# Second layer of a feed-forward by seven block products for eight, with sums on GpSimd

## The chip, the core and the metric

The kernel runs on one core of a Trainium2 chip. A core has TensorE (PE: matmuls, with weight loads of its own, PEld), VectorE (DVE), ScalarE (ACT), GpSimd (POOL) and SyncE (SP), which here issues the DMAs. The metric is device time in microseconds (us), lower is better. Each engine takes its instructions in the order in which the program holds them, and waits on semaphores for the other engines.

## What is computed

Chunked attention (8 batches, 8 heads, 576 tokens, chunks of 64) makes 4608 tokens of 512 numbers; a two-layer feed-forward follows, which is most of the work:

```python
scores = scale * np.matmul(q_c, k_c.transpose(0, 1, 2, 4, 3))   # per chunk of 64
attn = softmax(scores)
x = np.matmul(attn, v_c)  # 4608 tokens x 512
h = x @ w_in              # 512 x 2048
g = h - np.tanh(h)
return g @ w_out          # 2048 x 512
```

All is in float32. The kernel splits each operand of a matmul into a high and a low part and adds three products (high by high, high by low, low by high).

## The kernel before

The tokens are cut into nine **groups** of four tiles of 128 tokens (`SIZES`; the code's `g` runs from 0 to 8, and "the fourth group" is `g` = 3). The hidden width of 2048 is cut into 16 **chunks** of 128. A step of a group is one chunk: `gemm1` makes h of the chunk, transposed (hidden width on the partitions, 512 tokens along the free side), in 12 matmuls of 512 columns into one bank `ph` of two; `shrink` makes g and its two parts: ACT tanh into `t` (L465), DVE `h - tanh` (L466), ACT the high part `gh` (L472), DVE the low part `gl` (L473); `gemm2`, two steps later (`LAG`), multiplies the parts by the chunk's 128 rows of w_out, 12 matmuls of 512 columns, into the four banks `po`, which sum over the 16 chunks. `finish` scales `po` into tiles and stores them.

Groups 0 and 1 work on operands in fp32r. In groups 1 and 2 `convert` makes fp16 parts of the weights of both layers; from group 2 on both layers run on fp16. While a group's feed-forward runs, the attention of the next group is spread between its steps (`interleaved`): splits of q, k and v (L295 on ACT, L296 on DVE), score products (L306), maximum and difference (L319, L320), exponents (L321), sums (L327), normalising (L331), parts (L337, L338), a DMA that transposes, value products (L306), and the parts of the next `x` (L358, L359). The largest entries of the group after next are found by L105 on ACT (twice) and L122 on DVE, and spread over the partitions by an all-reduce on POOL (L112), whose result sets the scales of the next splits (L116 to L118).

The order on PE and SP of the very first stretch is written out by hand (`PLAN`); all else is ordered by the scheduler of the framework, from its own estimates of durations and from the order in which the code is written. What it puts down is fixed: each engine then runs its list in order.

## Time and profile before

| what | value |
|---|---|
| median of 3 runs | 846.0 us (844.26 to 846.85) |
| the profiled execution | 847.15 us, of which the span from first to last instruction is 845.4 us |
| granted clock of TensorE | 1.000 |
| PE busy | 836.3 us, 99% of the span |
| DVE busy | 527.1 us, 62% |
| ACT busy | 450.1 us, 53% |
| POOL busy | 4.1 us, in 15 instructions |

PE is busy when a matmul is in its pipeline, so 99% says that matmuls follow each other without holes, not that each runs at its best. The rows that the argument needs stand in the prediction.

### The profile page before, as it was taken

Reading aid. Unit: us, or ns where it says so; the run is one execution under the profiler, and the core shown is the slowest. Engines: PE = TensorE matmul, PEld = TensorE weight load, DVE = VectorE, ACT = ScalarE, POOL = GpSimd, SP = SyncE. Lnnn points to the kernel's source line nnn. Section 1 sums busy time; section 2 is a strip of 40 time slices with the busy share of each in tenths; the row PEclk is TensorE's granted clock in tenths of the full one; section 3 lists DMA queues with packets and bytes.
Section 4 is the critical chain, followed back from the end, with each engine's and each line's share of the span. In section 5 each row is a group of like instructions: output and inputs, shape, how many; then the busy total and the mean of one; then the engine's idle time right before and its main releaser. Section 6 shows DMA issues by size and latency. Waiting matters only on the chain.

```text
span 845.4 us, 15479 instructions
## 1 busy us (share of the span) xinstructions
PE 836.3 (99%) x6509; PEld 470.6 (56%) x6509; DVE 527.1 (62%) x811; ACT 450.1 (53%) x755; POOL 4.1 (0%) x15
## 2 busy tenths in 40 slices
PE   9999999999999999999999999999999999999998
PEld 6888777888844444444444444444444444444443
DVE  5897896877978754656465656564656474533222
ACT  6798785865978543644363446344634353333222
POOL 0000000000000000000000000000000000000000
PEclk9999999999999999999999999999999999999999
DMA  9885345221223131203130322132122101110001
GB/s 231 238 220 159 104 146 199 75 51 51 51 101 76 31 73 73 75 27 76 74 76 26 77 75 70 32 76 75 52 51 20 57 2 26 20 55 4 0 1 50
DMA packets 61382, 62.87 MB, mean 74 GB/s; under 512 B 32640, under 2 KB 40832, under 8 KB 61312
## 3 DMA queue, kind: packets, MB, share of 16 engines
q1 hardware_dynamic: 61312, 61.88, 26.5%
q8 instruction: 51, 0.84, 0.4%
q14 instruction: 19, 0.16, 0.1%
HBM read 45.09 MB, written 9.44 MB: 64 GB/s over the span
## 4 chain that ended last, share of the span: by engine, by line
PE 90%; DVE 5%; ACT 3%; issue 1%; DMA 0%; SPq 0%; POOL 0%; ACTq 0%; DVEq 0%
PE po L486 42%; PE ph L457 41%; PE psa L306 3%; PE psa L192 2%; PE psa L240 2%; DVE w L140 1%; DVE w L141 1%; PE ph L553 1%; ACT wl L417 1%; DVE wl L146 0%; DMA k<-kE 0%; PE psa L153 0%; DVE t L469 0%; DVE gl L478 0%; ACT wl L418 0%
## 5 line engine op out<-in xcount | busy, mean ns | idle before, releaser
L457 PE MATMUL ph<-xh,wl 128*128 128x512 f16 (+2 forms) x1404 | 324.1, 378 | 1.0 <-DVE t L466 1.0
L486 PE MATMUL po<-wl,gh 128*128 128x512 f16 (+1 forms) x968 | 300.3, 381 | 0.0
L457 PEld LDWEIGHTS <-wl 128*128 128x128 f16 x1260 | 122.3, 98 | 147.5 <-issue 1.3
L486 PE MATMUL po<-wl,gl 128*128 128x512 f16 x420 | 159.2, 379 | 0.0
L472 ACT ACTIVATE gh<-t,to_g 128x512 f16<-128x512 f32 x112 | 80.7, 720 | 134.9 <-PE po L486 96.0
L465 ACT ACTIVATE t<-ph,sig 128x512 f32<-128x512 f32 x112 | 76.8, 686 | 138.5 <-PE ph L457 138.1
L466 DVE SCALAR_TENSOR_TENSOR t<-ph,sig,t 128x512 f32<-128x512 f32 x112 | 83.9, 749 | 106.2 <-ACT t L465 106.2
L473 DVE SCALAR_TENSOR_TENSOR gl<-t,to_g,gh 128x512 f16<-128x512 f32 x112 | 83.9, 750 | 104.0 <-ACT gh L472 104.0
L486 PEld LDWEIGHTS <-gh 128*128 128x128 f16 x896 | 86.7, 98 | 103.4
L486 PEld LDWEIGHTS <-gl 128*128 128x128 f16 x448 | 43.8, 98 | 52.9
L486 PE MATMUL po<-wh,gh 128*128 128x512 f32 (+1 forms) x184 | 67.8, 393 | 0.7 <-ACT gh L477 0.7
L486 PE MATMUL po<-wh,gl 128*128 128x512 f32 (+1 forms) x156 | 60.7, 394 | 0.0
L457 PE MATMUL ph<-xh,wh 128*128 128x512 f32 (+1 forms) x144 | 36.8, 376 | 1.1 <-ACT wh L145 1.0
L457 PE MATMUL ph<-xl,wh 128*128 128x512 f32 (+1 forms) x144 | 35.4, 367 | 0.0
L306 PEld LDWEIGHTS <-wh 64*64 64x64 f16 x2688 | 24.5, 106 | 11.6 <-issue 11.6
L457 PEld LDWEIGHTS ph<-xh,wh 128*128 128x128 f32 x144 | 24.8, 188 | 6.9 <-ACT wh L145 2.5
L478 DVE TENSOR_TENSOR gl<-t,gh 128x512 fp32r<-128x512 f32 (+1 forms) x36 | 22.6, 629 | 9.7 <-ACT gh L477 7.3
L457 PEld LDWEIGHTS ph<-xh,wl 128*128 128x128 f32 x144 | 25.2, 188 | 5.3 <-DVE wl L146 0.6
L457 PEld LDWEIGHTS ph<-xl,wh 128*128 128x128 f32 x144 | 25.4, 188 | 4.8
L468 ACT ACTIVATE t<-ph 128x512 f32<-128x512 f32 (+1 forms) x36 | 19.7, 548 | 15.0 <-PE ph L457 14.8
L486 PEld LDWEIGHTS po<-wh,gh 128*128 128x128 f32 x128 | 24.1, 188 | 6.5 <-ACT gh L477 1.7
L486 PEld LDWEIGHTS po<-wh,gl 128*128 128x128 f32 x128 | 23.9, 188 | 6.3 <-DVE gl L478 1.3
(120 smaller groups left out, 857.1 us busy)
## 6 DMA issues: line engine op xcount, KB each, us to landing
raw<-w_in SPq DMA_DIRECT2D x16, 512.0 KB, 4.3
raw<-w_out SPq DMA_DIRECT2D x16, 512.0 KB, 5.7
out<-wh SPq DMA_DIRECT2D x32, 256.0 KB, 2.1
rawk<-kL SPq DMA_DIRECT2D x28, 256.0 KB, 2.9
rawv<-vL SPq DMA_DIRECT2D x28, 256.0 KB, 3.0
xl<-qL SPq DMA_DIRECT2D x28, 256.0 KB, 2.9
qbd<-qE SPq DMA_DIRECT2D x16, 128.0 KB, 5.6
k<-kE SPq DMA_DIRECT2D x8, 256.0 KB, 6.1
```

The lines of the kernel that those rows point to most:

```text
L140: nc.vector.scalar_tensor_tensor(out=w, in0=low, scalar=29, in1=w, op0=ALU.logical_shift_right, op1=ALU.bitwise_or)
L192: nc.tensor.matmul(ps[:, h, :], lhsT=d["q"][:, h // 2, :, h % 2], rhs=d["k"][:, h, :], start=True, stop=True)
L240: nc.tensor.matmul(ps[:, hp, cs], lhsT=d["v"][:, hp, :, c], rhs=d["aT"][:, hp, cs], start=True, stop=True)
L306: nc.tensor.matmul(ps(c, e, hp)[u * D:(u + 1) * D], lhsT=stationary(a, r, e, hp, u), rhs=moving(b, r, e, hp, u), start=(i == 0), stop=(i = ...
L457: nc.tensor.matmul(ph, lhsT=self.weight(fc, 0, a)[:, kc * P:(kc + 1) * P], rhs=x[b][:, kc, cols], start=(k == 0), stop=(k == 3 * KC - 1))
L465: nc.scalar.activation(t, ph, AF.Tanh, scale=self.sig)
L466: nc.vector.scalar_tensor_tensor(out=t, in0=ph, scalar=self.sig, in1=t, op0=ALU.mult, op1=ALU.subtract)
L468: nc.scalar.activation(t, ph, AF.Tanh)
L472: nc.scalar.activation(gh, t, AF.Copy, scale=self.to_g)
L473: nc.vector.scalar_tensor_tensor(out=gl, in0=t, scalar=self.to_g, in1=gh, op0=ALU.mult, op1=ALU.subtract)
L478: nc.vector.tensor_sub(gl, t, gh)
L486: nc.tensor.matmul(self.po[t], lhsT=gg[a][:, ts], rhs=self.weight(fc, 1, b), start=(fc == 0 and i == 0), stop=(fc == FC - 1 and i == 2))
```

## The change

From the fourth group on (`FAST` = 3) the second layer takes blocks of two token tiles by two chunks (`j` and `j` + 8) by two halves of the output width. Such a 2 x 2 by 2 x 2 product of blocks, eight block products before, is made from **seven** products of sums of blocks (of Strassen's kind). A step is now a **unit**: a pair of token tiles `b` (two to a group) and a pair of chunks `j` (eight), 16 units to a group as there were 16 steps. `gemm1` does the same multiplications in 24 matmuls of 256 columns; `gemm2` does 21 matmuls of 256 columns (seven products by three) where the same share of work was 12 of 512. Three units (`FAST_LAG`), not two, lie between a unit's `gemm1` and its `gemm2`, four around the change of a pair of tiles.

Between them `shrink` does more: tanh (L584, ACT) and difference (L585, DVE) on 512 columns as before, then three instructions on POOL that make the sums of g's blocks (L586 on 256 columns, L587 on 128, L588 on 256), then the high part of all seven blocks (L589, ACT) and the low part (L590, DVE), each on 896 columns. `u`, which the POOL works in, has two buffers; `gh` and `gl` have five.

After the last `j` of a pair, `finish` joins the seven results: two instructions on ACT, six on DVE of 256 columns (L620), two on POOL (L625, L631).

The sums of w_out's blocks are made in the third group (`g` = 2): `combine(j)` does six sums on POOL, three on 512 columns and three on 256, `shorten(j)` splits the four results on ACT (L454) and DVE (L455). `combine(j)` writes where w_out's own parts lie, so it waits until the third group's `gemm2` has read them. That group now takes its chunks in pairs (0, 8, 1, 9, ...), and its second layer runs on fp32r again, since no fp16 parts of w_out are made.

The order changes at three places that matter below.

First POOL. Its list in the kernel before, from the making of the identity matrix at the start (`ident`) to its last all-reduce (`xtop`: the largest entries of q, k and v of a group, seven of them); `ISA` stands for an all-reduce, or, where it has no operands, for a load of the code that the next instruction needs:

```order
masks.py:197 MEMSET ident 128x128
masks.py:199 ISA
masks.py:199 AFFINE_SELECT ident<-ident 128x128
L405 ISA
L405 ISA whole<-sums_102 128x16
L112 ISA wtop<-both 128x2
L112 ISA xtop<-sums 128x3 x7
```

After the change, around the all-reduce that falls into the fourth group (the same stands around each of the next three):

```order
L586 TENSOR_TENSOR xl<-xl 128x256
L587 TENSOR_TENSOR xl<-xl 128x128
L588 TENSOR_TENSOR xl<-xl 128x2x128
L114 ISA
L114 ISA xtop<-sums 128x3
L586 ISA
L586 TENSOR_TENSOR xl<-xl 128x256
L587 TENSOR_TENSOR xl<-xl 128x128
L588 TENSOR_TENSOR xl<-xl 128x2x128
```

The all-reduce used to be alone on POOL, with its code in place from the first; now it stands between the sums of one unit (ahead of it) and of the next (behind it), with a load of code ahead of it and another behind it.

Second DVE in the fifth group, where the scores of the group's first half arrive. The kernel before (L466 and L473 are the two instructions of a step, the rest is attention):

```order
L473 SCALAR_TENSOR_TENSOR gl<-t,to_g,gh 128x512
L466 SCALAR_TENSOR_TENSOR t<-ph,sig,t 128x512
L319 TENSOR_REDUCE mx<-psa 128x16
L296 SCALAR_TENSOR_TENSOR wh_1697<-xl,to,wh_1696 128x1024
L320 TENSOR_TENSOR s<-psa,mx 128x2x8x64
L473 SCALAR_TENSOR_TENSOR gl<-t,to_g,gh 128x512
L296 SCALAR_TENSOR_TENSOR wh_2623<-rawk,to,wh_2622 128x1024
L327 TENSOR_REDUCE sm<-s 128x16
L466 SCALAR_TENSOR_TENSOR t<-ph,sig,t 128x512
L328 TENSOR_SCALAR sm<-sm 128x16
L329 RECIPROCAL sm<-sm 128x16
```

The same place after the change (L585 and L590 are the two instructions of a unit; L298, L322 and L329 to L340 are the attention's L296, L320 and L327 to L338 of before):

```order
L590 SCALAR_TENSOR_TENSOR gl<-xl,to_g,gh 128x896
L322 TENSOR_TENSOR s<-psa,mx 128x2x8x64
L298 SCALAR_TENSOR_TENSOR wh_1697<-xl,to,wh_1696 128x1024
L585 SCALAR_TENSOR_TENSOR xl<-ph,sig,t 128x512
L329 TENSOR_REDUCE sm<-s 128x16
L330 TENSOR_SCALAR sm<-sm 128x16
L331 RECIPROCAL sm<-sm 128x16
L332 TENSOR_SCALAR sm<-sm 128x16
L590 SCALAR_TENSOR_TENSOR gl<-xl,to_g,gh 128x896
L333 TENSOR_TENSOR s<-s,sm 128x1024
L340 TENSOR_TENSOR a<-s,a 128x2x512
L585 SCALAR_TENSOR_TENSOR xl<-ph,sig,t 128x512
```

The list has the same shape: L590 of a unit stands ahead of L585 of the next, and rows of attention stand between the two.

Third ACT in the fourth group, around that all-reduce, before (L105 finds the largest entries) and, behind it, after (L107 is that line, L584 and L589 are tanh and high part of a unit, L297 and L360 the splits and the parts of `x`):

```order
L465 ACTIVATE t<-ph,sig 128x512
L105 ACTIVATE wh_2630,sums<-xl 128x2048
L472 ACTIVATE gh<-t,to_g 128x512
L105 ACTIVATE wh_2630,sums<-rawk 128x2048
L337 CAST a<-s 128x2x512
L465 ACTIVATE t<-ph,sig 128x512
L472 ACTIVATE gh<-t,to_g 128x512
```

```order
L589 ACTIVATE gh<-xl,to_g 128x896
L107 ACTIVATE a,sums<-xl 128x2048
L107 ACTIVATE a,sums<-rawk 128x2048
L584 ACTIVATE t<-ph,sig 128x512
L297 ACTIVATE wh_1696<-xl,to 128x1024
L297 ACTIVATE a<-rawk,to 128x1024
L360 ACTIVATE xh<-psa 128x4x128
L297 ACTIVATE wh_1698<-rawv,to 128x1024
L584 ACTIVATE t<-ph,sig 128x512
L360 ACTIVATE xh<-psa 128x4x128
L589 ACTIVATE gh<-xl,to_g 128x896
```

The two L107 now follow each other ahead of a unit's tanh, and two tanh (L584) stand ahead of the two high parts (L589), which wait for POOL.

The diff, cut:

```diff
+FAST = 3
+FAST_LAG = 3
...
+        def combine(self, j):
+            (h1, l1), (h2, l2) = ([t.bitcast(F32) for t in wt[fc][1]] for fc in (j, j + FC // 2))
+            names = [(a, 1, fc) for fc in (j, j + FC // 2) for a in "hl"]
+            free = self.free
+            w1 = place_of(*free[0], F32)
+            nc.gpsimd.tensor_add(w1, h1, l1)
+            w2 = place_of(*names[0], F32)
+            nc.gpsimd.tensor_add(w2, h2, l2)
+            x, y = (place_of(*n, F32) for n in names[1:3])
+            nc.gpsimd.tensor_sub(x, w2, w1)
+            nc.gpsimd.tensor_add(y[:, :HD], w1[:, :HD], w1[:, HD:])
+            nc.gpsimd.tensor_add(y[:, HD:], w2[:, :HD], w2[:, HD:])
+            nc.gpsimd.tensor_add(w1[:, HD:], w1[:, :HD], w2[:, HD:])
+            self.sums[j] = w1, x, y, w2[:, HD:]
+            self.dest[j] = [names[3], free[1], free[2]]
+            if j % 2 == 0:
+                self.last = place_of(*free[3])
+            self.free = [free[0], *names[:3], *free[3 + (j % 2 == 0):]]
+        def shorten(self, j):
+            to = self.to[:, 1:2]
+            parts = [place_of(*n).rearrange("p (a n) -> p a n", a=2) for n in self.dest[j]]
+            parts.append(self.last[:, (j % 2) * DM:(j % 2 + 1) * DM].rearrange("p (a n) -> p a n", a=2))
+            for t, part in zip(self.sums.pop(j), parts, strict=True):
+                nc.scalar.activation(part[:, 0], t, AF.Copy, scale=to)
+                nc.vector.scalar_tensor_tensor(out=part[:, 1], in0=t, scalar=to, in1=part[:, 0], op0=ALU.mult, op1=ALU.subtract)
+            a, b, c, d = parts
+            left, right = slice(0, HD), slice(HD, DM)
+            fast_w[j] = {1: a[:, :, right], 2: a[:, :, left], 3: b[:, :, right], 4: b[:, :, left], 5: d, 6: c[:, :, left], 7: c[:, :, right]}
...
     class FeedForward:
...
-            self.half = g > 1, g > 1
+            self.half = g > 1
...
+        BANKS = ((4, 5), (1, 7), (2, 3), (6,))
+        SUM = {7: 0, 3: 1, 4: 2, 6: 3, 5: 4, 2: 5, 1: 6}
+        def __init__(self, pools):
+            self.pools, self.queue, self.units, self.po = pools, [], 0, None
+            u = xpool.tile([P, KC, MOST], F32R, name="xl").bitcast(F32).rearrange("p a n -> p (a n)")
+            self.u = [u[:, i * 8 * P:i * 8 * P + 7 * P].rearrange("p (s n) -> p s n", n=P) for i in range(2)]
+            tiles = [ffn.tile([P, MOST], F32R, name=f"g{a}").bitcast(F16) for _ in range(2) for a in "hl"] + g_tiles
+            self.g = [[t[:, :7 * P].rearrange("p (s n) -> p s n", n=P) for t in tiles[2 * i:2 * i + 2]] for i in range(FAST_LAG + 2)]
...
+        def gemm1(self, b, j):
+            self.ph = ps_h.tile([P, 4, P], F32, name="ph")
+            for f in range(2):
+                fc = j + f * FC // 2
+                k = 0
+                for w, v in ((0, 0), (1, 0), (0, 1)):
+                    for kc in range(KC):
+                        rhs = self.x[v][:, kc, 2 * b * P:2 * (b + 1) * P].rearrange("p (t n) -> p t n", n=P)
+                        nc.tensor.matmul(self.ph[:, 1 - f::2, :], lhsT=half_w[fc][:, w, kc * P:(kc + 1) * P], rhs=rhs, start=(k == 0), stop=(k == 3 * KC - 1))
+                        k += 1
+        def shrink(self, b, j):
+            sig, to = self.powers[:2]
+            t = ffn.tile([P, MOST], F32, name="t", bufs=3).rearrange("p (s n) -> p s n", n=P)
+            u, (gh, gl) = self.u[self.units % 2], self.g[self.units % len(self.g)]
+            self.units += 1
+            nc.scalar.activation(t, self.ph, AF.Tanh, scale=sig)
+            nc.vector.scalar_tensor_tensor(out=u[:, :4], in0=self.ph, scalar=sig, in1=t, op0=ALU.mult, op1=ALU.subtract)
+            nc.gpsimd.tensor_add(u[:, 4:6], u[:, 1:3], u[:, 0:4:3])
+            nc.gpsimd.tensor_add(u[:, 6], u[:, 1], u[:, 2])
+            nc.gpsimd.tensor_sub(u[:, 0:4:3], u[:, 0:2], u[:, 2:4])
+            nc.scalar.activation(gh, u, AF.Copy, scale=to)
+            nc.vector.scalar_tensor_tensor(out=gl, in0=u, scalar=to, in1=gh, op0=ALU.mult, op1=ALU.subtract)
+            self.queue.append((b, j, gh, gl, self.powers, self.row + 2 * b * P))
...
+        def gemm2(self):
+            b, j, gh, gl, powers, row = self.queue.pop(0)
+            if j == 0:
+                self.po = [self.pools[i // 2].tile([P, DM], F32, name=f"po{i}") for i in range(4)]
+            place = {m: self.po[i][:, k * HD:(k + 1) * HD] for i, ms in enumerate(self.BANKS) for k, m in enumerate(ms)}
+            w = fast_w[j]
+            opening = {ms[0] for ms in self.BANKS}
+            for part, ops in ((gh, (0, 1)), (gl, (0,))):
+                for m in place:
+                    for o in ops:
+                        first = j == 0 and part is gh and o == 0 and m in opening
+                        nc.tensor.matmul(place[m], lhsT=part[:, self.SUM[m]], rhs=w[m][:, o], start=first, stop=(j == FC // 2 - 1 and part is gl), skip_group_check=True)
+            if j == FC // 2 - 1:
+                self.finish(b, place, powers, row)
+        def finish(self, b, m, powers, row):
+            undo, minus = powers[2:]
+            e, f, r = post
+            e4, e5 = e[:, :HD], e[:, HD:]
+            e1, p = f[:, :HD], f[:, HD:]
+            q, r = r[:, :HD], r[:, HD:]
+            oa, ob = outs[2 * b], outs[2 * b + 1]
+            def add(out, in0, scalar, in1):
+                nc.vector.scalar_tensor_tensor(out=out, in0=in0, scalar=scalar, in1=in1, op0=ALU.mult, op1=ALU.add)
+            nc.scalar.activation(e, self.po[0], AF.Copy, scale=undo)
+            nc.scalar.activation(e1, m[1], AF.Copy, scale=undo)
+            add(p, m[7], undo, e4)
+            nc.gpsimd.tensor_sub(q, e1, e5)
+            add(ob[:, :HD], m[2], undo, e4)
+            add(r, m[2], minus, e1)
+            add(oa[:, HD:], m[3], minus, e5)
+            add(r, m[3], minus, r)
+            add(ob[:, HD:], m[6], minus, r)
+            nc.gpsimd.tensor_add(oa[:, :HD], p, q)
+            for t, o in enumerate((oa, ob)):
+                nc.sync.dma_start(out=out[row + t * P:row + (t + 1) * P, :], in_=o)
+        def run(self, g, x, at):
+            self.group(g, x)
+            waited = False
+            for s in range(2 * FC // 2):
+                unit = divmod(s, FC // 2)
+                self.gemm1(*unit)
+                self.shrink(*unit)
+                for f in at.pop(2 * s, []):
+                    f()
+                if len(self.queue) > FAST_LAG:
+                    if self.first_next() and not waited:
+                        waited = True
+                    else:
+                        waited = False
+                        self.gemm2()
+                        if len(self.queue) > FAST_LAG and not self.first_next():
+                            self.gemm2()
+                for f in at.pop(2 * s + 1, []):
+                    f()
+            for k in sorted(at):
+                for f in at[k]:
+                    f()
...
+        if g < FAST:
+            if g == FAST - 1:
+                for j in range(FC // 2):
+                    at[4 * j + 7].append(lambda j=j: half.combine(j))
+                    k = 4 * j + 9
+                    (at if k < 2 * (FC + LAG) else over)[k].append(lambda j=j: half.shorten(j))
+            order = range(FC) if g < FAST - 1 else [j + f * FC // 2 for j in range(FC // 2) for f in range(2)]
+            ff = FeedForward(g, x)
+            ff.room(ps_o1, range(2))
+            ff.room(ps_o2, range(2, SIZES[g]))
+            ff.run([(fc, 0, SIZES[g]) for fc in order], at)
+            continue
+        if g == FAST:
+            for fs in over.values():
+                for f in fs:
+                    f()
+            post.extend(place_of(*n, F32) for n in half.free[:3])
+            g_tiles.extend(place_of(*n) for n in half.free[3:5])
+            fast = Fast((ps_o1, ps_o2))
+        fast.run(g, x, at)
+    fast.drain()
```

More of the change, by code (lines that the diff above doesn't have):

```diff
@@ L389, in __init__ @@
             self.to, self.back = (const.tile([P, 2], F32, name=n) for n in ("to_w", "from_w"))
+            self.free, self.sums, self.dest = [], {}, {}
         def powers(self):
@@ L409, in powers, with convert @@
             nc.vector.tensor_single_scalar(self.to_h.bitcast(U32), self.to_h.bitcast(U32), EXPONENT, op=ALU.bitwise_and)
-        def convert(self, part, fc, place):
-            half_w[part][fc] = place.rearrange("p (a n) -> p a n", a=2)
-            (h, l), (h16, l16), to = wt[fc][part], (half_w[part][fc][:, i] for i in range(2)), self.to[:, part:part + 1]
+        def convert(self, fc, place):
+            half_w[fc] = place.rearrange("p (a n) -> p a n", a=2)
+            (h, l), (h16, l16), to = wt[fc][0], (half_w[fc][:, i] for i in range(2)), self.to[:, 0:1]
             h, l = h.bitcast(F32), l.bitcast(F32)
@@ L423, in power_of @@
         def power_of(self, g):
-            sig, to, undo = (const.tile([P, 1], F32, name=n, bufs=2) for n in ("sig", "to_g", "undo_g"))
+            sig, to, undo, minus = (const.tile([P, 1], F32, name=n, bufs=2) for n in ("sig", "to_g", "undo_g", "minus_g"))
             nc.vector.tensor_mul(sig, from_x[g], self.back[:, 0:1])
-            nc.vector.scalar_tensor_tensor(out=to, in0=to_x[g], scalar=4.0, in1=self.to_h, op0=ALU.mult, op1=ALU.mult)
+            nc.vector.scalar_tensor_tensor(out=to, in0=to_x[g], scalar=2.0, in1=self.to_h, op0=ALU.mult, op1=ALU.mult)
@@ L438, in __init__ @@
             self.g, self.x, self.queue, self.po = g, x, [], []
-            self.half = g > 1, g > 1
+            self.half = g > 1
             if g > 1:
-                self.sig, self.to_g, self.undo_g = half.power_of(g)
+                self.sig = half.power_of(g)[0]
         def weight(self, fc, part, i):
-            return half_w[part][fc][:, i] if self.half[part] else wt[fc][part][i]
+            return half_w[fc][:, i] if self.half and part == 0 else wt[fc][part][i]
         def room(self, pool, tiles):
@@ L603, in attn_ffn_kernel @@
     late = ctx.enter_context(tc.tile_pool(name="att", bufs=1, side="right", reuse_waits="tile"))
-    att, half = Late(late), Half(late)
+    att, half, over = Late(late), Half(late), defaultdict(list)
     for g in range(1, NG):
         x, nx = nx, new_half_x() if g + 1 < NG else None
-        ff = FeedForward(g, x)
-        ff.room(ps_o1, range(2))
-        ff.room(ps_o2, range(2, SIZES[g]))
         at = interleaved(att, g + 1, nx) if nx else {}
@@ L614, in attn_ffn_kernel @@
             for fc in range(FC):
-                at[2 * fc + 1].append(lambda fc=fc: half.convert(0, fc, place_of("l", 0, fc - 1) if fc else first_place))
+                at[2 * fc + 1].append(lambda fc=fc: half.convert(fc, place_of("l", 0, fc - 1) if fc else first_place))
             def more(k):
-                t = [place_of("h", 0, fc) for fc in (range(4) if k == 0 else range(4, 13))]
                 if k == 0:
+                    t = [place_of("h", 0, fc) for fc in range(4)]
                     att.q16, att.v16 = t[0:2], t[2:4]
@@ L623, in more @@
                 else:
[L624 to L626 removed]
+                    outs.extend(place_of("h", 0, fc, F32) for fc in range(4, 8))
+                    g_tiles.extend(place_of("h", 0, fc) for fc in range(8, 12))
+                    half.free = [("h", 0, 12), ("h", 0, 13), ("h", 0, 14), ("h", 0, 15)]
             at[8].insert(0, lambda: more(0))
@@ L629, in attn_ffn_kernel @@
             at[2 * FC + 2].append(lambda: more(1))
-        for fc in range(FC):
-            if g == (1 if fc < AHEAD else 2):
-                k = 2 * FC + 2 * (LAG - AHEAD + fc) - 3 if g == 1 else 2 * (fc - AHEAD) + 1
-                at[k].append(lambda fc=fc: half.convert(1, fc, place_of("l", 1, fc - 1) if fc else place_of("h", 0, 13)))
-        ff.run([(fc, 0, SIZES[g]) for fc in range(FC)], at)
+        if g < FAST:
[10 more added lines that the diff above has]
+            continue
```

45 lines of the change are left out of this document (21 added, 24 removed).

## Prediction

> **What bounds the kernel now.** I read the totals first, then the chain that ended last, then windows of one group each, then single steps.
>
> ```profile
> PE 836.3 (99%) x6509; PEld 470.6 (56%) x6509; DVE 527.1 (62%) x811; ACT 450.1 (53%) x755; POOL 4.1 (0%) x15
> ...
> PE 90%; DVE 5%; ACT 3%; issue 1%; DMA 0%; SPq 0%; POOL 0%; ACTq 0%; DVEq 0%
> ```
>
> PE is the bound by both. The windows view (window, its length, then busy time of each engine) shows it by stage, here for the fifth group and the last:
>
> ```profile
> 410.40:497.40 87.00, 87.00 (x769) 40.81 (x768) 50.71 (x71) 40.56 (x53) 0.37 (x1) 1.00 0.24 62
> 758.30:845.40 87.10, 83.08 (x385) 37.46 (x383) 26.30 (x35) 24.20 (x35) 0.00 (x0) 1.00 0.06 24
> ```
>
> A group takes 87.0 us, in all of which PE is busy; the last, without attention, 83.1 us and an end of 4. One step in the timeline (start, duration):
>
> ```profile
> 500.21 0.69 ACT L465 ACTIVATE t<-ph,sig 128x512 f32<-128x512 f32 x1 [2.55 <-PE ph L457]
> 500.93 0.75 DVE L466 SCALAR_TENSOR_TENSOR t<-ph,sig,t 128x512 f32<-128x512 f32 x1 [2.10 <-ACT t L465]
> 501.72 0.72 ACT L472 ACTIVATE gh<-t,to_g 128x512 f16<-128x512 f32 x1 [0.82 <-DVE t L466]
> 502.47 0.75 DVE L473 SCALAR_TENSOR_TENSOR gl<-t,to_g,gh 128x512 f16<-128x512 f32 x1 [0.79 <-ACT gh L472]
> ...
> 507.78 2.75 PE L457 MATMUL ph<-xh,wl 128*128 128x512 f16 x12
> ...
> 510.46 0.98 PE L306 MATMUL psa<-wh,wh 64*64 64x64 f16 x96
> ```
>
> Twelve matmuls take 2.75 us; less the last one's length of 0.38, the eleven intervals are 0.216 us each. A step is 24 of them, 5.2 us. Its chain on the other engines runs from 500.93, DVE's first, to 503.22, the end of DVE's second: 2.3 us. DVE takes the next step's L466 only behind L473, so this is the shortest period that ACT and DVE allow. **2.3 of 5.2 us: that cover hides the attention's work on ACT and DVE today**, and it is what the change spends.
>
> **PE's share: a gain of 18 us if nothing else waited.** A unit has 24 + 21 matmuls of 256 columns. No fp16 matmul of 256 columns stands in the trace. Halving 0.216 gives 0.108 as the lower bound; the fp32r ones give the upper:
>
> ```profile
> 28.22 0.64 PE L457 MATMUL ph<-xh,wl 128*128 128x256 f32 x4
> 28.69 0.64 PE L457 MATMUL ph<-xl,wh 128*128 128x256 f32 x4
> ...
> 142.31 1.09 PE L457 MATMUL ph<-xh,wh 128*128 128x512 f32 x4
> ...
> 148.86 1.10 PE L457 MATMUL ph<-xh,wl 128*128 128x512 f32 x4
> ...
> L457 PEld LDWEIGHTS <-wl 128*128 128x128 f16 x1260 | 122.3, 98 | 147.5 <-issue 1.3
> L457 PEld LDWEIGHTS ph<-xh,wl 128*128 128x128 f32 x144 | 25.2, 188 | 5.3 <-DVE wl L146 0.6
> ```
>
> There four take 0.47, 0.118 each, behind weight loads of 188 ns; and 512 columns take 6.55 / 28 = 0.234. I take 0.110, since the fp16 load is half as long (98 ns) and a halved interval still covers it. A unit is then 45 x 0.110 = 4.95 us and a group 79.2 + 4 x 0.98 of attention = 83.1 for 87.0. Six groups give 5 x 3.9 + 3.9 = 23 us. The third group loses 192 x (0.23 - 0.216) = 3 us, since its second layer goes back to fp32r, and the end grows by some 2 (below). That leaves 18.
>
> **The unit's chain: 2.3 becomes 4.6 us.** Durations on 896 columns lie on the line between 512 and 1024; POOL has only small rows:
>
> ```profile
> L473 DVE SCALAR_TENSOR_TENSOR gl<-t,to_g,gh 128x512 f16<-128x512 f32 x112 | 83.9, 750 | 104.0 <-ACT gh L472 104.0
> L296 DVE SCALAR_TENSOR_TENSOR wh<-rawv,to,wh 128x1024 f16<-128x1024 f32 x14 | 18.0, 1283 | 8.2 <-ACT wh L295 8.2
> ...
> L472 ACT ACTIVATE gh<-t,to_g 128x512 f16<-128x512 f32 x112 | 80.7, 720 | 134.9 <-PE po L486 96.0 <-DVE t L466 18.5 <-DVE sums L123 17.0
> L295 ACT ACTIVATE wh<-rawv,to 128x1024 f16<-128x1024 f32 x14 | 16.1, 1147 | 3.8 <-PE psa L306 3.8
> ...
> 0.33 0.10 POOL L670 MEMSET const-uint8-127<- 128x1 uint8 x1
> 0.72 0.20 POOL masks.py:197 MEMSET ident<- 128x128 f32 x1 [0.29 <-POOLq L670]
> 7.91 0.28 POOL masks.py:199 TENSOR_SCALAR_AFFINE_SELECT ident<-ident 128x128 f32<-128x128 f32 x1 [6.99 <-issue]
> L469 DVE TENSOR_TENSOR t<-ph,t 128x256 f32<-128x256 f32 x8 | 3.4, 421 | 0.0
> ```
>
> L590 comes to 0.75 + 0.75 x 0.53 = 1.15, L589 to 0.72 + 0.75 x 0.43 = 1.04. On POOL one column costs (0.20 - 0.10) / 128 = 0.8 ns to write and 1.4 ns to read and write, so reading costs 0.6, and two inputs 2.0 to 2.1 ns; with 0.10 to start, three instructions on 640 columns take 640 x 2.07 + 0.3 = **1.62 us** (an estimate). Lower bound: DVE's pace, 0.42 for 256 columns and 0.29 for 128 (less 128 at L473's slope), 1.13. Upper: each input priced as a whole read and write, 640 x 2.9 + 0.3 = 2.15. The Trainium skill ("GPSIMD Engine Reference", section "Elementwise — side-by-side cycle accounting") speaks against putting such sums there: it gives 4497 ns for 2048 columns, twice the Vector engine. By that figure three instructions would take about 1.4 us and the sum below would end near 888; no run here shows it yet.
>
> The chain is 0.75 + 1.62 + 1.04 + 1.15 and four hand-overs of 0.03 to 0.04 (500.93 + 0.75 to 501.72), less 0.08 that back-to-back instructions overlap (below): 4.6 us, for PE's 4.95. Three units of lag hide its length, but its period is what counts: L590 still stands ahead of the next L585. What cover is left is 0.35 a unit, 5.6 a group.
>
> **What stands between the chain's links.** The order above shows rows of attention between L590 and the next L585. In the holes of 2.3 us they were free; on the chain each counts whole:
>
> ```profile
> L331 DVE TENSOR_TENSOR s<-s,sm 128x1024 f32<-128x1024 f32 x14 | 17.1, 1225 | 0.5
> L359 DVE SCALAR_TENSOR_TENSOR xh<-psa,xh 128x512 f16<-128x512 f32 x28 | 19.2, 684 | 0.9 <-ACT xh L358 0.9
> L122 DVE TENSOR_REDUCE sums<-rawv 128x1 f32<-128x2048 f32 x7 | 16.0, 2286 | 7.9 <-DMA rawv<-vL 7.9
> ...
> L337 ACT CAST a<-s 128x1024 f16<-128x1024 f32 x14 | 14.5, 1039 | 6.4 <-DVE s L331 6.4
> L105 ACT ACTIVATE wh<-rawk 128x2048 uint8<-128x2048 f32 x6 | 11.4, 1908 | 1.9 <-DMA rawk<-kL 1.2 <-ACT gh L472 0.7
> ...
> 469.16 0.74 DVE L466 SCALAR_TENSOR_TENSOR t<-ph,sig,t 128x512 f32<-128x512 f32 x1
> 469.81 1.28 DVE L296 SCALAR_TENSOR_TENSOR wh<-rawk,to,wh 128x1024 f16<-128x1024 f32 x1
> ```
>
> Back to back, an instruction begins 0.08 to 0.09 before the other's recorded end, so L298 counts 1.20, passes over 1024 columns 1.14, L361 0.60, and L620 (256 columns, as L469) 0.34. In a group of after's order: two joins' L620 and, behind one, two passes 1.4 + 4.0; a pass with a split 2.3; L333, its high part on ACT and L340 3.4; L298 1.2; two L361 round a split 2.4; a late L340 with small ones 1.4; two L107 ahead of a tanh 3.4 (2 x 1.9, less 0.4 of cover); and three splits and two L361 between two L585, which wait for the all-reduce, 3.5. L124 (L122 before) fills a hole of 2.7 us with its 2.3, but waits for a load that SP can issue only behind the split of the same buffer: 7.9 / 7 = 1.1, all of it late. Sum 24 us.
>
> **Loads of code on POOL.** The row at 7.91 shows 6.99 us without a visible instruction ahead of the first one that needed code. In after's order POOL loads before the all-reduce and again behind it, 14 us in the fourth to seventh groups. The first falls into POOL's idle time and the ACT work above; the second holds a unit's sums, which lag and two tanh ahead of two L589 hide but for some 1.2 us. The Trainium skill ("GPSIMD Engine Reference", section "Instruction dispatch") names about 6 us for the first call of freshly loaded code; the row is longer, and no run here shows yet whether later loads cost as much.
>
> A group with attention thus takes 16 x 4.6 + 24 + 1.2 = **99 us for 87**. The fourth begins with a lead of three units and no join, +8; the fifth to seventh +12 each; the eighth, which prepares no further group, +4; the last is PE's, 80 for 83, -3.
>
> **The third group and its end.**
>
> ```profile
> 235.31 2.76 PE L457 MATMUL ph<-xh,first_place 128*128 128x512 f16 x12
> ...
> 326.97 0.75 DVE L466 SCALAR_TENSOR_TENSOR t<-ph,sig,t 128x512 f32<-128x512 f32 x1 [2.10 <-ACT t L465]
> ...
> 542.50 0.37 POOL L112 PARTITION_ALL_REDUCE xtop<-sums  x1 [86.76 <-DVE sums L123]
> ```
>
> POOL holds the all-reduce behind `combine(5)`, which waits for the twelfth `gemm2`: 235.3 + 14 x 2.6 + 12 x 2.8 + 2.9 = 308. Its five last sums (512 columns 1.16, 256 0.63) end at 312, a load at 319, all-reduce, load at 327, then `combine(6)` and `combine(7)` of 5.4 each: 337.5. Their parts (L454, L455) stand ahead of the first unit's tanh and L585, which therefore ends near 340 instead of 327.7: **+12**. DVE meanwhile waits in L118 for the all-reduce, with the last chunk's parts queued behind it, for which PE waits some 4 us; that lies within the 12.
>
> **What I cost at nothing.** `shorten` has 32 instructions on ACT and 32 on DVE, as `convert` had for w_out; the third group's 2.3 of 5.4 us a step hides them, but for the last eight of each, which are in the 12. On SP stores and loads keep their number; behind a pair's stores, which wait for the join, stand a group's second transposes, but the join ends a unit or so ahead of them. If that cover went, the value products would wait as long as the join is late.
>
> **The end.**
>
> ```profile
> 841.00 0.38 PE L486 MATMUL po<-wl,gl 128*128 128x512 f16 x1
> 841.41 0.75 DVE L510 TENSOR_SCALAR wh<-po,undo_g 128x512 f32<-128x512 f32 x1 [0.55 <-PE po L486]
> ```
>
> Behind the last matmul stood 0.75; now come one of 0.69, six L620 and POOL's last, 3.2: +2.
>
> **The sum.** 12 + 8 + 36 + 4 - 3 + 2 = +59 on the profiled execution's 847.15: 906. The median of the runs lies 1.1 lower: **905 us**.
>
> **Rivals.** (1) *The chain stays covered and PE remains the bound*: 846 - 18 = 828, the faster side. The place is the chain between two L585; it decides once the three sums take under some 0.7 us ((83 - 24) / 16 = 3.7, less 3.0 for the rest). For it: 99% PE and a lag of three units. Against it: 0.20 to 0.28 us for a single 128 columns on POOL. 10%. (2) *Short sums or free loads*: at 1.13 us a unit loses 0.49, a group 7.8, four and a half groups 35, and `combine` 4: 866; later loads at nothing take 1.2 from four groups and some 8 from the third group's end: 892. 20% for 858 to 882. (3) *Long sums*, 2.15, or POOL held up by DVE's work beside it: 80 chain-bound units x 0.53 and slower `combine`, 5: 952; 11% for 928 to 958. (4) *The change does not save on PE*: weight loads, now one per 256 columns at 98 ns each, set the pace. The bound shifts only above (99 - 3.9) / 720 = 0.132 a matmul; at 0.14 it gives five groups of 105 and one of 101: 846 + 12 + 90 + 18 + 2 = 968. The fp32r row, 0.118 with a load of 188 ns, speaks against. With the longest sums, above 958: 5%. No change within 0.3%: 2%.
>
> **How the numbers follow.** My forecast (882 to 928) has 52%, so slower holds 52 + 20 + 11 + 5 = 88%; a difference under 0.3% a measurement here cannot tell from none. The range 858 to 958 leaves out rival 1, no change and the highest: 17%.
>
> **What would show it.** Right: PE with idle time of some 16 us in each of the fifth to seventh groups, released by DVE's L585; the three sums of a unit at 1.6 us; POOL silent for 14 us around each `xtop`; the first L585 near 340. Wrong: fp16 matmuls of 256 columns above 0.13 apart (rival 4), POOL's sums under 0.7 us or group periods of 83 us (rival 1), or no gap behind `xtop` (rival 2).

## The result, and the profile after

The changed kernel takes **953.9 us** (median of 4 runs, 953.27 to 954.5) for 846.4 of before on the same chip (844.26 to 846.89): a ratio of **1.128**, 95% interval 1.125 to 1.130. The forecast was 905 us, with a range to 958. The direction and the mechanism held; the loss is 107 us where 59 were forecast, and the time lies above the 882 to 928 us that the forecast gave 52%, in the stretch that it gave to rival 3 (11%).

The totals of the profiled execution (span 952.2 us, before 845.4), and the row of PE's granted clock:

```profile
PE 847.2 (89%) x8525; PEld 694.3 (73%) x8525; DVE 606.1 (64%) x878; ACT 472.9 (50%) x767; POOL 268.9 (28%) x375
...
PEclk9999999999999979999998999999999999999999
```

PE issues 2016 matmuls more, works 11 us longer and is no longer the bound: 89% for 99%. The windows view for the fifth group and for the last with its end (window, length, then the busy time of PE, PEld, DVE, ACT and POOL, the clock, the DMA share and GB/s):

```profile
451.80:556.40 104.60, 88.80 (x1094) 75.29 (x1094) 61.40 (x83) 44.66 (x54) 34.54 (x53) 0.95 0.18 52
864.60:952.20 87.60, 79.38 (x720) 70.14 (x718) 35.58 (x50) 28.32 (x37) 34.64 (x54) 0.99 0.05 19
```

No engine is full in the fifth group: PE idles 15.8 of 104.6 us, DVE and POOL far more. That is how a chain of waits looks. It shows in the timeline of an undisturbed unit in the last group (start, duration; in the timelines of several engines PE's rows are left out, but where PE is the point):

```profile
889.50 0.74 DVE L585 SCALAR_TENSOR_TENSOR xl<-ph,sig,t 128x512 f32<-128x512 f32 x1
890.33 0.72 POOL L586 TENSOR_TENSOR xl<-xl 128x256 f32<-128x256 f32 x1 [3.00 <-DVE xl L585]
891.01 0.45 POOL L587 TENSOR_TENSOR xl<-xl 128x128 f32<-128x128 f32 x1
891.42 0.73 POOL L588 TENSOR_TENSOR xl<-xl 128x256 f32<-128x256 f32 x1
892.18 1.04 ACT L589 ACTIVATE gh<-xl,to_g 128x896 f16<-128x896 f32 x1 [3.20 <-POOL xl L588]
893.13 0.67 ACT L584 ACTIVATE t<-ph,sig 128x512 f32<-128x512 f32 x1
893.26 1.15 DVE L590 SCALAR_TENSOR_TENSOR gl<-xl,to_g,gh 128x896 f16<-128x896 f32 x1 [3.01 <-ACT gh L589]
...
894.33 0.74 DVE L585 SCALAR_TENSOR_TENSOR xl<-ph,sig,t 128x512 f32<-128x512 f32 x1
```

Apart from L584, the next unit's tanh, each row begins within 0.1 us of the end of the one before it, on three engines in turn, and the next unit's L585 stands behind L590: **4.82 us** from one L585 to the next (889.50 to 894.33). That tanh is done by 893.80, and its result waits.

The L585 rows give the time by stages. They are 96, one a unit, sixteen a group:

```profile
L585 DVE SCALAR_TENSOR_TENSOR xl<-ph,sig,t x96: 656/743/751, 349.3 to 939.3; 128x512 f32<-128x512 f32 x96
```

| stretch, between the ends of the groups' first L585 (before: L466) | before | after | more | forecast |
|---|---|---|---|---|
| start to the fourth group's | 327.7 | 350.1 | +22.4 | +12 |
| fourth group | 87.0 | 101.7 | +14.7 | +8 |
| fifth, sixth, seventh | 87.0 each | 104.6, 104.9, 105.7 | +54.2 | +36 |
| eighth | 87.0 | 97.6 | +10.6 | +4 |
| last, to its last one | 72.5 | 75.4 | +2.9 | -3 |
| end | 10.3 | 12.2 | +1.9 | +2 |

The sum is 106.7, all but 0.1 of what the spans differ by.

### The profile page after: what moved, and what is told of

Same layout as the page of the kernel before. It is cut to its first block, busy times and chain, and to the rows that moved or that the text cites. A ratio compares the mean times of both kernels' runs of the same rounds, so it can differ in the third digit from the quotient of the medians.

```text
span 952.2 us, 19954 instructions
## 1 busy us (share of the span) xinstructions
PE 847.2 (89%) x8525; PEld 694.3 (73%) x8525; DVE 606.1 (64%) x878; ACT 472.9 (50%) x767; POOL 268.9 (28%) x375
## 3 DMA queue, kind: packets, MB, share of 16 engines
q1 hardware_dynamic: 61312, 61.88, 22.4%
## 4 chain that ended last, share of the span: by engine, by line
PE 30%; DVE 28%; POOL 16%; ACT 12%; DMA 7%; issue 5%; SPq 2%; ACTq 0%; DVEq 0%; POOLq 0%
PE ph L495 10%; PE po L519 10%; DVE xl L585 5%; POOL xl L586 5%; POOL xl L588 5%; ACT wh L589 4%; DMA s<-a 4%; PE po L607 4%; DVE wh L590 4%; PE ph L576 3%; POOL xl L587 3%; ACT gh L589 3%; DVE gl L590 3%; DVE wh L298 2%; DVE a L298 1%
## 5 line engine op out<-in xcount | busy, mean ns | idle before, releaser
L576 PE MATMUL ph<-xh,wl 128*128 128x256 f16 x2160 | 262.2, 280 | 38.5 <-DVE xl L585 38.4
L576 PEld LDWEIGHTS <-wl 128*128 128x128 f16 x2160 | 215.8, 100 | 72.5 <-issue 42.2
L586 POOL TENSOR_TENSOR xl<-xl 128x256 f32<-128x256 f32 x96 | 69.5, 724 | 346.9 <-DVE xl L585 290.9
L590 DVE SCALAR_TENSOR_TENSOR wh<-xl,to_g,wh 128x896 f16<-128x896 f32 x57 | 66.5, 1167 | 130.0 <-ACT wh L589 130.0
L607 PEld LDWEIGHTS <-wh 128*128 128x128 f16 x1197 | 120.7, 101 | 36.3 <-issue 18.9
L589 ACT ACTIVATE wh<-xl,to_g 128x896 f16<-128x896 f32 x57 | 59.4, 1042 | 172.6 <-POOL xl L588 167.3
L607 PE MATMUL po<-wl,wh 128*128 128x256 f16 x642 | 107.2, 277 | 10.9 <-DVE wh L620 7.4
L607 PE MATMUL po<-wh,wh 128*128 128x256 f16 x555 | 105.8, 288 | 4.3 <-DVE wh L620 4.3
L590 DVE SCALAR_TENSOR_TENSOR gl<-xl,to_g,gh 128x896 f16<-128x896 f32 x39 | 46.3, 1187 | 84.7 <-ACT gh L589 84.7
L589 ACT ACTIVATE gh<-xl,to_g 128x896 f16<-128x896 f32 x39 | 40.6, 1042 | 117.9 <-POOL xl L588 112.7
L519 PE MATMUL po<-wh,gh 128*128 128x512 f32 x192 | 79.4, 414 | 4.4 <-ACT gh L510 4.4
L585 DVE SCALAR_TENSOR_TENSOR xl<-ph,sig,t 128x512 f32<-128x512 f32 x96 | 70.9, 739 | 18.5 <-ACT t L584 18.5
L495 PE MATMUL ph<-xh,wl 128*128 128x512 f16 (+2 forms) x324 | 77.0, 375 | 4.3 <-DVE t L504 3.2
L519 PE MATMUL po<-wh,gl 128*128 128x512 f32 x192 | 76.3, 401 | 0.5 <-DVE gl L511 0.4
L519 PE MATMUL po<-wl,gh 128*128 128x512 f32 x192 | 76.0, 396 | 0.0
L588 POOL TENSOR_TENSOR xl<-xl 128x256 f32<-128x256 f32 x96 | 70.5, 735 | 0.0
L607 PEld LDWEIGHTS <-gh 128*128 128x128 f16 x546 | 54.2, 100 | 19.0 <-issue 11.9
L584 ACT ACTIVATE t<-ph,sig 128x512 f32<-128x512 f32 x96 | 64.4, 671 | 1.0 <-PE ph L576 1.0
L607 PE MATMUL po<-wl,gh 128*128 128x256 f16 x292 | 45.4, 276 | 7.0 <-DVE wh L620 4.7
L587 POOL TENSOR_TENSOR xl<-xl 128x128 f32<-128x128 f32 x96 | 48.3, 504 | 0.0
```

The source lines that it names most:

```text
L495: nc.tensor.matmul(ph, lhsT=self.weight(fc, 0, a)[:, kc * P:(kc + 1) * P], rhs=x[b][:, kc, cols], start=(k == 0), stop=(k == 3 * KC - 1))
L519: nc.tensor.matmul(self.po[t], lhsT=gg[a][:, ts], rhs=self.weight(fc, 1, b), start=(fc == 0 and i == 0), stop=(fc == FC - 1 and i == 2))
L576: nc.tensor.matmul(self.ph[:, 1 - f::2, :], lhsT=half_w[fc][:, w, kc * P:(kc + 1) * P], rhs=rhs, start=(k == 0), stop=(k == 3 * KC - 1))
L584: nc.scalar.activation(t, self.ph, AF.Tanh, scale=sig)
L585: nc.vector.scalar_tensor_tensor(out=u[:, :4], in0=self.ph, scalar=sig, in1=t, op0=ALU.mult, op1=ALU.subtract)
L586: nc.gpsimd.tensor_add(u[:, 4:6], u[:, 1:3], u[:, 0:4:3])
```

## The experiments

Theory A is the prediction's: POOL's three sums cost time because L590 stands ahead of the next unit's L585, so what counts is the period of the chain and not the work on any engine. Theory B: POOL and DVE hold one another up, or POOL's loads of code do, in whatever order. Unless rounds are given, a time is of one run beside the kernel before (845.7 to 847.1 in those calls).

**pipe: the chain cut by the order of the code.** `rest()` issues the L589 and L590 that the unit before left `ready`.

```diff
-            nc.scalar.activation(gh, u, AF.Copy, scale=to)
-            nc.vector.scalar_tensor_tensor(out=gl, in0=u, scalar=to, in1=gh, op0=ALU.mult, op1=ALU.subtract)
+            self.rest()
+            self.ready = u, gh, gl, to
```

> Edit: the high and low parts (L589, L590) of a unit are issued behind the next unit's L585 instead of ahead of it; the three sums stay on POOL, nothing is removed. Theory A (the period: the three sums are late only because L590 stands ahead of the next L585, so that tanh, difference, sums, high and low part of one unit must all end before the next begins): the chain between two L585 falls from 4.82 us to about 2, PE becomes the bound again in the fourth to ninth groups, from one group's first L585 to the next's some 83 to 88 us instead of 98 to 106, the whole 850 to 875 us. Theory B (POOL and DVE hold one another up, or the loads of code on POOL do, whatever the order): DVE's and POOL's work is the same, so less than 30 us go, above 920 us.

946.8 us. By the numbers that is theory B's case; but the period was still 4.82, so I asked first whether the chain had been cut at all. My first answer, a wait for a whole tile, led to the next run.

**pipe_two: as pipe, with two tiles for the unit's blocks.**

```diff
-            self.u = [u[:, i * 8 * P:i * 8 * P + 7 * P]... for i in range(2)]
+            self.u = [t[:, :7 * P]... for t in (u, late.tile([P, 7 * P], F32, name="u", bufs=1))]
```

> Edit: as in the run before with the later order (L589 and L590 of a unit behind the next unit's L585), but the two buffers of a unit's blocks are two tiles; so far they were two parts of one tile. In that run's trace the high part began 0.04 us behind the end of the NEXT unit's last sum (561.17 behind 561.13), and the period stayed 4.82 us. Theory A2: the wait is for the whole tile, so the order alone could not take the sums off the path; with two tiles they lie beside PE's work, the groups come to 86 to 90 us (the run without sums: 86), and the whole to 862 to 885 us. Theory B (POOL and DVE hold one another up whatever the order): above 930 us.

944.4 us: no change, so theory A2's case did not come. But two tiles have two names, and its timeline now tells which unit a row belongs to:

```profile
557.17 0.74 DVE L585 SCALAR_TENSOR_TENSOR u<-ph,sig,t 128x512 f32<-128x512 f32 x1
558.00 0.73 POOL L586 TENSOR_TENSOR u<-u 128x256 f32<-128x256 f32 x1 [3.00 <-DVE u L585]
...
559.85 1.04 ACT L597 ACTIVATE wh<-u,to_g 128x896 f16<-128x896 f32 x1 [3.21 <-POOL u L588]
...
560.93 1.15 DVE L598 SCALAR_TENSOR_TENSOR wh<-u,to_g,wh 128x896 f16<-128x896 f32 x1 [3.01 <-ACT wh L597]
...
562.00 0.75 DVE L585 SCALAR_TENSOR_TENSOR xl<-ph,sig,t 128x512 f32<-128x512 f32 x1
```

Difference, sums, high and low part (here L597 and L598) are all of `u`, one unit, and only then comes the next L585, to `xl`. The scheduler had put the pieces back into the old order. Both runs say nothing on A or B, and the wait that A2 was to explain is explained by the order alone.

**pin: the order held.**

```diff
+            with tc.issue_after(tanh.ins), tc.issue_after(diff.ins):
+                self.rest()
```

> Edit: the later order of the run pipe (a unit's L589 and L590 behind the next unit's tanh and L585), this time held by two order-only edges per unit. In pipe and pipe_two the scheduler had put a unit's own high and low part back ahead of the next unit's L585 (with two tiles the trace shows it by name: u<-u on POOL, then wh<-u on ACT and DVE, then the next L585 to xl), so both ran the old order, and their times said nothing on theory A; the theory of the whole tile is dropped. Theory A: with the order held the three sums lie beside other work, groups of 86 to 92 us instead of 98 to 106, PE near its floor (the run without sums: 862 us); the whole 862 to 885 us. Theory B (POOL and DVE hold one another up, DVE's work with that is the bound): DVE is busy some 63 of 105 us a group, but if it rises with the overlap and the groups stay above 98: above 930 us.

888.6 us, 65 less than the changed kernel, with the same instructions. This time the order did change, as an undisturbed unit of the last group shows (L598 and L599 are high and low part here):

```profile
827.90 1.03 ACT L598 ACTIVATE gh<-xl,to_g 128x896 f16<-128x896 f32 x1
828.03 0.75 DVE L585 SCALAR_TENSOR_TENSOR xl<-ph,sig,t 128x512 f32<-128x512 f32 x1 [2.41 <-ACT t L584]
828.86 0.72 POOL L586 TENSOR_TENSOR xl<-xl 128x256 f32<-128x256 f32 x1 [2.25 <-DVE xl L585]
828.96 1.57 DVE L599 SCALAR_TENSOR_TENSOR gl<-xl,to_g,gh 128x896 f16<-128x896 f32 x1 [0.18 <-ACT gh L598]
829.54 1.30 POOL L587 TENSOR_TENSOR xl<-xl 128x128 f32<-128x128 f32 x1
830.81 0.72 POOL L588 TENSOR_TENSOR xl<-xl 128x256 f32<-128x256 f32 x1
...
832.94 0.75 DVE L585 SCALAR_TENSOR_TENSOR xl<-ph,sig,t 128x512 f32<-128x512 f32 x1 [2.41 <-ACT t L584]
```

High and low part are those of the unit before, since this unit's sums begin only at 828.86; from one L585 to the next it is now PE's 4.91 us, and L585 waits for its tanh. The total is 4 us above A's range, and the groups take 91.4, 92.7, 91.6, 92.7 and 81.5 us for 101.7, 104.6, 104.9, 105.7 and 97.6: **theory A holds for the greater part**. It is not the 862 of the floor below. Part of what is left is theory B's, and two groups of the listing by lines show it (busy us, mean ns):

```profile
L586 POOL TENSOR_TENSOR xl<-xl 128x256 f32<-128x256 f32 x96 | 105.8, 1102 | 258.2 <-DVE xl L585 228.7 <-DVE xh L361 14.3 <-DVE wh L298 7.7
...
L599 DVE SCALAR_TENSOR_TENSOR wh<-xl,to_g,wh 128x896 f16<-128x896 f32 x57 | 78.6, 1379 | 27.9 <-ACT wh L598 27.8
```

In the changed kernel they had 724 and 1167 ns (L599 is L590 there). Side by side the sums and the low parts get in one another's way, as the 1.57 of L599 and the 1.30 of L587 above show (1.15 and 0.45 alone); the alternation had kept them apart.

**no_sums: the floor.** The three sums are left out, and the blocks that they would fill hold zeros.

```diff
-            nc.gpsimd.tensor_add(u[:, 4:6], u[:, 1:3], u[:, 0:4:3])
-            nc.gpsimd.tensor_add(u[:, 6], u[:, 1], u[:, 2])
-            nc.gpsimd.tensor_sub(u[:, 0:4:3], u[:, 0:2], u[:, 2:4])
```

> Edit: the three sums of a unit (L586 to L588) are left out, and blocks 4 to 6 of each unit's sums hold zeros set once; everything else, the 21 matmuls of a unit too, stays. This is the floor that PE sets with seven products. Theory A: the chain is 3.0 us a unit, 16 x 3.0 + 27 = 75 us a group, under PE's 16 x 4.91 + 4 x 0.98 = 82.5; so 952 - 82 (what the fourth to last groups lost) - 26 (what PE saves there) = 844 to 850 us, all of it lost or won against before in the third group's end. If PE itself is slower than its intervals of 0.109 us say (its clock or its weight loads), it stays above 870.

861.8 us, 12 above the forecast's upper end: the first L585 ends at 350.3, as in the changed kernel, but the groups take 84.9, 86.0, 86.2, 86.4 and 78.8 us for 82.5. In the windows view of the fifth PE is busy 83.1 us, as worked out; 3 us of waits are left even without the sums.

```profile
435.20:521.20 86.00, 83.10 (x1106) 73.52 (x1105) 59.69 (x83) 44.66 (x54) 3.30 (x5) 1.00 0.22 63
```

So the sums cost 92 us in this kernel, and without them seven products win 1 us of 87 in a group with attention.

**dve_sums: the three sums on DVE, in the changed kernel's order.**

```diff
-            nc.gpsimd.tensor_add(u[:, 4:6], u[:, 1:3], u[:, 0:4:3])
+            nc.vector.tensor_add(u[:, 4:6], u[:, 1:3], u[:, 0:4:3])
...
```

> Edit: the three sums of a unit (L586 to L588) on DVE instead of POOL, in the changed kernel's order; the weights' sums of the third group stay on POOL. Theory A: a unit's chain loses 1.8 us and gains three instructions of some 0.2 to 0.4 on DVE (about 1.0): 4.0 us for 4.82, 16 x 4.0 + 27 of attention's rows = 91 us a group for 104.7; five such groups and the last give -65: about 890 us. The third group's end stays 22 us late. Theory B (mutual hold-up): DVE's passes over two inputs, too, get their durations of before (L333 1.22 for 1.42) and the loads inside the groups go, some 3 and 7 us a group more: about 850.

879.9 us. The period of an undisturbed unit is 3.92 us, 0.9 less, and the fourth to seventh groups take 87.8 to 91.3. This lies between the two cases: the chain's part was forecast right (91 us a group), and 10 us more went than that case has, which was not followed up.

**pin_dve: both.** The edits of pin and of dve_sums.

> Edit: as pin, with the three sums on DVE. Theory A: DVE's work of 74 us a group fits under PE's 83, the run without sums gives the floor of 862; 862 to 872 us. If DVE's queue is the limit (waits for all-reduce, DMA and PE stand in it in order), no better than the 880 of dve_sums. If pin is slower than this by 5 us or more, the overlap of POOL's sums with DVE's passes has a price; if pin is faster, DVE's room is worth more than that.

876.3 us, the fourth to seventh groups 87.2 to 90.4: 4 us above theory A's range and 4 below the other's 880. It is 12 us faster than pin, so POOL's overlap with DVE costs more than the sums themselves on DVE; it beats dve_sums by 3.6 only, which single runs don't tell apart (the four of pin_combine below lie 6.6 us apart). DVE's queue, where waits for the all-reduce, the loads and PE stand in order, is the likelier limit here; no run shows it apart.

**pipe_two_dve:** the sums on DVE with the order of pipe_two, which the scheduler is free to undo.

> Edit: as pipe_two, and the three sums on DVE. Theory A2: with the sums on DVE alone the chain was 3.9 us a unit and the whole 880 us; off the path it is near the run without sums, 862 to 870 us, although DVE then works 74 of some 87 us in a group. If DVE's own work is the bound, it stays at 878 or above. Against pipe_two: if POOL's sums and DVE's passes over two inputs slow one another, pipe_two is the slower by 5 to 20 us; if not, the faster.

897.0 us, 17 more than dve_sums: the fifth to seventh groups take 94.4 to 96.0 us. Another order came out, and a worse one. By the number this is the case of 878 or above, but it shows nothing on DVE's own work, since the order that both cases assumed wasn't run; why this one is worse was not followed up.

**no_reduce_4: POOL without its loads of code** (`alone` holds for the fifth to ninth groups).

```diff
-        nc.gpsimd.partition_all_reduce(top, sums, channels=P, reduce_op=bass_isa.ReduceOp.max)
+        if alone:
+            nc.vector.tensor_copy(top, sums)
+        else:
+            nc.gpsimd.partition_all_reduce(top, sums, channels=P, reduce_op=bass_isa.ReduceOp.max)
```

> Edit: the maximum across partitions on POOL (xtop) is left out for the fifth to ninth groups' attention, the last five of seven; a copy on DVE takes its place, so each partition has its own power of two. With it POOL loads no other code from the third group's end on. Theory A with the forecast's own terms: 1.2 us in each of four groups and 8 at the third group's end, 13 in all: 941 us. Rival: each load holds the chain for its whole 7 us, two per all-reduce: 14 us at the third group's end and 7 to 14 in each of four groups: 885 to 910.

959.6 us: not faster at all, against both. The first L585 ends at 347.4, 2.6 earlier, and four groups are 1.7 to 2.5 us longer. Around an all-reduce in the changed kernel, POOL's timeline has two silent stretches:

```profile
535.50 0.72 POOL L588 TENSOR_TENSOR xl<-xl 128x256 f32<-128x256 f32 x1
542.46 0.39 POOL L114 PARTITION_ALL_REDUCE xtop<-sums  x1 [6.24 <-ACT a L107]
549.85 0.71 POOL L586 TENSOR_TENSOR xl<-xl 128x256 f32<-128x256 f32 x1 [7.00 <-DVE wh L298]
550.54 0.44 POOL L587 TENSOR_TENSOR xl<-xl 128x128 f32<-128x128 f32 x1
...
551.63 0.72 POOL L586 TENSOR_TENSOR xl<-xl 128x256 f32<-128x256 f32 x1
```

6.24 and 7.00 us, and then the sums of two units in a row. The first stretch doesn't show how long a load takes: it ends 0.13 us behind the second of two L107 of 1.91 us on ACT, whose result the all-reduce needs and for which DVE waits anyway. The second does: the L585 that this L586 follows was done at 543.69. (In pin the all-reduces of the fourth to seventh groups start 0.5 to 0.6 us behind that result, and their first stretches are 5.7 to 6.0 us.) During the second stretch DVE works on the three splits. Without the loads the sums meet those splits: in the fifth group the second and the third sum beside them took 1.44 and 1.71 us for 0.45 and 0.72.

**combine_dve: the weights' sums of the third group on DVE.**

```diff
-            nc.gpsimd.tensor_add(w1, h1, l1)
+            nc.vector.tensor_add(w1, h1, l1)
...
```

> Edit: the sums of the weights' blocks (L434 to L441, 8 times six instructions, third group) on DVE instead of POOL, all else as in the changed kernel. First L585 of the fourth group ended at 350.1 there (before the change 327.7; without the all-reduces 347.4). Theory C: the end is late because the last two chunks' sums take 6.6 to 8.5 us each on POOL, the last of them behind PE's last matmul of the group; on DVE some 3 us each: first L585 at 338 to 343, the whole 942 to 947 us. Rival: DVE has no room, its queue holds the unit's own L511 up and PE with it: 350 or later, 954 us or more.

941.3 us, first L585 at 336.8: 13.3 of the 22.4 us at the third group's end are POOL's. Its timeline in the changed kernel, with DVE's and PE's rows:

```profile
331.33 2.89 POOL L434 TENSOR_TENSOR wh<-wh,wl 128x512 f32<-128x512 f32 x1 [7.16 <-DVE t L504]
...
341.24 1.26 POOL L434 TENSOR_TENSOR wh<-wh,wl 128x512 f32<-128x512 f32 x1 [1.62 <-DVE wl L455]
...
346.69 1.17 POOL L441 TENSOR_TENSOR wh<-wh,wh 128x256 f32<-128x256 f32 x1
...
348.64 0.75 DVE L455 SCALAR_TENSOR_TENSOR wl<-wh,to_w,wl 128x512 f16<-128x512 f32 x1 [0.24 <-ACT wl L454]
349.31 0.75 DVE L585 SCALAR_TENSOR_TENSOR xl<-ph,sig,t 128x512 f32<-128x512 f32 x1
...
350.11 2.29 PE L576 MATMUL ph<-xh,wl 128*128 128x256 f16 x10 [7.62 <-DVE xl L585]
```

The last chunk's sums run from 341.24 to 347.86, its parts behind them, and the first L585 behind those; PE, whose last matmul of the third group began at 336.84, waits 7.62 us.

**all_dve and pin_combine: whether the two ends add.** combine_dve with pipe_two_dve, and with pin.

> Edit: pipe_two_dve and combine_dve together; POOL keeps the all-reduces and the joins' two instructions. If the two terms add: the time of pipe_two_dve less what combine_dve saves, 852 to 862 us, still no better than the kernel before, since a group of 86 saves only 1 us of 87 and the third group's end still costs 10 or more. If they overlap: that of pipe_two_dve.

> Edit: as pin, and the weights' sums of the third group on DVE. combine_dve took the first L585 of the fourth group from 350.1 to 336.8 and the whole from 953.9 to 941.3; if that adds, the time of pin less 12: 850 to 873 us, slower than the kernel before (846) by what the third group's end still costs (9 us) and what its groups gain (1 us each).

all_dve: 882.2 us, 14.9 less than pipe_two_dve (its forecast started from a better pipe_two_dve). pin_combine, 3 rounds: 874.0 us, 1 above its range, ratio 1.033 (1.029 to 1.037), 14.6 less than pin. combine_dve had won 12.7; the terms add, within what single runs tell.

**final: the best of each.**

> Edit: pin_dve, with the weights' sums of the first seven chunks on DVE, those of the eighth on POOL, and the eighth chunk's short parts (L454, L455) held by order edges behind the second unit of the fourth group instead of ahead of its first. Theory: the terms add. pin_dve 876, less 12.6 (combine_dve against the changed kernel), less 1 to 2 more for the first L585, which then waits for nothing but its 24 matmuls (336 for 338 us): 861 to 863 us. If the third group's end overlaps with what pin_dve already won: 868 or more. In either case slower than the kernel before, by about 2%: groups of 86 to 90 us for 87 win nothing, and the third group's end, about 9 us late, and the fp32r second layer in it are not won back.

861.5 us, ratio **1.018** (1.015 to 1.021) in 3 rounds: as forecast, and still slower than the kernel before. Its first L585 ends at 336.0 (+8.3), the groups take 86.0, 88.7, 88.8, 91.2, 82.4 and 73.7 (+3.3 in all), the end 13.7 us (+3.4): 15 us, the difference of the spans. No version that was run beats the kernel before.

## Why the prediction was right, and where it was too small

- **The mechanism: right.** "Its period is what counts: L590 still stands ahead of the next L585." pin, with every instruction kept, took back 65 of 107 us. Rival 1, that lag hides the chain, is out: 4.82 us between two L585 leave 0.1 of PE's 4.91 (in the last group, where PE's first-layer matmuls start at 889.25 and 894.16).
- **PE's matmuls: right.** 0.110 us was taken, the median interval is 0.109 (matmuls of L576 and L607); rival 4 is out. But the gain on PE hardly arrives: no_sums shows 86 us a group for 87, where the forecast had 83.1.
- **The chain, 4.6 forecast, 4.82 measured.** L589 and L590 came out as worked out, 1.04 and 1.15. The failed term is the sums: 1.62 forecast, 1.82 from 890.33 to 892.15. The slope was right ((0.72 - 0.45) / 128 = 2.1 ns a column); the start is 0.18 us and not 0.10, three times. At 16 units the 0.22 are 3.5 us a group. The Trainium skill's figure ("GPSIMD Engine Reference", section "Elementwise — side-by-side cycle accounting"), 4497 ns for 2048 columns, comes to 2.2 ns a column (an estimate). The slope agrees; for short rows the start has to be added.
- **Attention's rows, 25.2 forecast with the visible load, 27.5 measured** (104.6 less 16 x 4.82). The largest miss is the two L107 ahead of a tanh: the interval with them is 9.35 to 9.48 us, some 4.6 over the period, for 3.4. Chain and rows together are the 6 us by which each of the fifth to seventh groups, and the fourth and eighth, were under-estimated: 31 of the missing 48.
- **The third group's end, +12 forecast, +22.4 measured**: 10 of the 48. Two steps failed. "Its five last sums (512 columns 1.16, 256 0.63) end at 312": they end at 317.85, and `combine(6)` begins at 331.33 for 327. And "then `combine(6)` and `combine(7)` of 5.4 each: 337.5": undisturbed they take 6.6 us (341.24 to 347.86), with 1.26 for 512 columns where 1.16 was taken; beside DVE's work 8.3 (331.33 to 339.62). The second also waits 1.62 for a part of the first. The loads, forecast as some 8 of the 12, are worth 2.6 (no_reduce_4).
- **The last group, -3 forecast, +2.9 measured**: 6 of the 48. It was called PE's; with 4.82 against 4.91 the chain is as long, and two joins put 1.6 us each on it: 15 x 4.82 + 3.1 = 75.4. But this miss isn't the chain's: without the sums (no_sums), where PE doesn't wait there, this stretch and the end take 74.0 and 13.4 us, 87.4 for the 87.6 here and the 82.8 of before. Three units of lag put more of PE's work behind the group's first L585 (81.3 us in no_sums, 78.8 before); "80 for 83" counted a whole group's matmuls and not these. The other 2 us of the 4.6 stand behind the last matmul, as forecast for the end.
- **Loads of code: the sign came, the cost didn't.** POOL is silent for 13 to 14 us around each `xtop`, as forecast, and this costs nothing net. The load behind it takes as long as the first one did (7.0 to 7.3 us in the fourth to seventh groups, 6.99 before). For the first call of freshly loaded code the Trainium skill ("GPSIMD Engine Reference", section "Instruction dispatch") names about 6 us. What a load costs depends on what lies beside it.
- **PE's idle time: the size came, the releaser half.** 15.8 us in the fifth group, 16 forecast. The view of PE's waits there puts 8.7 us on L585; the others are the joins and attention's transposes, which come late with the chain (all of the run from the fourth group on):

```profile
PE ph L576 <- DVE xl L585: 39.8, 32, 7.6
PE po L607 <- DVE wh L620: 19.2, 21, 1.3
PE psa L308 <- DMA s<-a: 18.7, 17, 3.0
```

- **Rival 3 gave the time, 952, but not the way.** It had sums of 2.15, or POOL held up by DVE. The sums are 1.82, and in the changed kernel POOL's sums for the units are held up seldom: of 96 L587 five took 1.44 us and the others 0.45. Only the slower `combine` came as it said. The missing time is spread over four terms, each too small: that the total came out inside the range, near a rival with another cause, is in part luck.

## What to carry over

When work is moved to an idle engine, ask whether it lands between two instructions that another engine runs in order: then its whole length is added to the period, however idle the engine was, and lag doesn't help. To cut such a chain, look in the trace whether the order really changed, by the names of the buffers, before reading anything from the time. And sum a change that touches a whole loop with each term's upper bound too: here four shortfalls of one sign made nearly half of the loss.
